# Weighted values two units at a time, ahead of every second unit's scores, with the stage's work placed by a table

## The chip, the cores and the metric

The kernel runs on one core of one Trainium2 chip. The metric is the device time of one execution in microseconds. The core has five engines with a queue of instructions each, which they work off in order: TensorE (PE, matrix products; its weight loads are listed apart as PEld), VectorE (DVE), ScalarE (ACT), GpSimd (POOL) and SyncE (SP), which here issues all DMA transfers. Engines wait for each other by semaphores. Products land in PSUM, an accumulator memory of eight banks (0 to 7 in the code, `PS[:, bank, :]`); a bank has to be read out by ACT or DVE before PE may use it for something else.

## The reference

One sequence of 2048 rows of 512 numbers, in bfloat16. `xn` is the normalized `x`; an attention branch A and an MLP branch B both start from it, and the output is `x + A * silu(B)`.

```python
xn = _layernorm(x)
# A: 32 heads of 16; a row attends to itself and 7 earlier rows, 2 apart
W, dil = 8, 2
qkv = (xn @ wqkv)...                       # q, k, v per head
idx = pos[:, None] - (jnp.arange(W) * dil)[None, :]
logits = jnp.einsum("bhsd,bhswd->bhsw", q, kg) * Dh ** -0.5
attn = softmax(where(idx >= 0, logits, -1e9))
A = jnp.einsum("bhsw,bhswd->bhsd", attn, vg)... @ wo
# B
h = gelu(_layernorm(xn) @ w1)              # then shifted by 1 or 2 rows, by quarters of the columns
x1 = xn + h_shifted @ w2
B = x1 + gelu(_layernorm(x1) @ w3) @ w4    # w3: 512 x 1376, w4: 1376 x 512
return x + A * silu(B)
```

## The kernel before

Rows attend to rows of their own parity alone, so the rows are kept as two halves (`p` = 0, 1) of 1024 even or odd rows. The first 106 us load, normalize and project: queries, keys (`kM`), values, which are written to DRAM (`v_d`), and the MLP as far as the hidden activations (`h3a`, `h3b`). What the change touches is the stage behind that, a loop over `NU` = 18 units, nine to each half, of 114 rows each. The names in it:

- `scores(n)` (S in what follows): 32 products on row tiles 32*128 of TensorE into PSUM banks 0 to 3 (L682), then one `Exp` of ACT (L689) into `prob`. The next unit's scores need that Exp to be done.
- `band(n)`: DVE takes the minimum of `prob` with a mask (L694), which leaves the eight wanted keys of each row.
- `values(n)`: 32 products of `prob` with value rows on column tiles 128*32 (L708) into bank 4 (`O_ps`), 16 products for the softmax denominators into bank 5 (L718), and a copy of bank 4 by ACT into `oT` (L723). It runs for unit n-2, right behind the scores of unit n, until unit 15, where two units' values are caught up, each apart.
- `load_va(n)`: SP loads the unit's value rows from `v_d` into one of `NV` = 3 places of the tile `ring` (L671). A place is free once the values of three units ago are done. `ring` takes the memory of `w3_sb`, so the first loads come behind the last product with w3.
- `inverse()`, `write_rec(b)`, `read_rec(b, ...)`, `apply(b, ...)`: for a batch of four units DVE takes the reciprocal of the denominators (L730), SP writes it to DRAM (two transfers, L739) and reads it back spread over partitions (two, L742), and DVE multiplies `oT` with it (L755). They also lie on SP's one queue.
- `w4_take(k)`: k of the 176 products with `w4` (L820). Eleven of them make one `Group` for 128 rows: the group takes a bank from `free`, which starts as `[6, 7]`, at its first product and puts it back at its last; DVE adds the bank to `x1` (L833), ACT takes a tanh (L840) and DVE makes the gate of it (L842). TensorE's time between the small blocks is filled with these, by shares worked out from `W4`, `kept_back` and the unit's number.
- `small_g`: a group of four products in each unit, for the queries of the second half in units 0 to 7 (L851, copied by ACT at L857), later for the output product with `wo` (L877, copied at L884; `finals` then multiplies with the gate, L892, and adds to the output rows `xo`, L896). They use the banks of `free`, too.
- `load_xo`, `flush_stores`, `load_wo`: loads of `x` rows into `xo` (L522), stores of finished rows (L784), the load of `wo` (L781), all on SP's queue.

`pin` keeps every engine's instructions in the order in which the code issues them: what the loop issues first, its engine does first. Behind the loop stand the last unit's values, the last eight products with `w4`, and the output groups 1 to 7 of the second half.

Of the kernel before, what the change touches and what calls it, by code (L numbers as in the profile page):

```python
# [8 lines left out]
AF = mybir.ActivationFunctionType  # L9
# [11 lines left out]
def kernel(  # L21
# [19 lines left out]
    def pin(ins):  # L41

        return tc.keep_in_program_order(ins)

    P = 128
    S = 2048
# [77 lines left out]
    load_x(2, 0, 2)  # L124
    load_x(2, 2, 2)
    w2_sb = b4([P, ND, D], "w2_sb")
    WS = 5664
    w3_sb = wpl.tile([P, WS], BF16, name="w3_sb", tag="w")[:, 0 : ND * F].rearrange("p (dt f) -> p dt f", f=F)
    w4_sb = wpl.tile([P, WS], BF16, name="w4_sb", tag="w")[:, 0 : NF * D].rearrange("p (ft n) -> p ft n", n=D)
    pin(ACT.preload_act_table_set("sqrt_and_others"))  # L130
# [81 lines left out]
    class Norm:  # L212
# [24 lines left out]
        def apply(self, lo, hi):  # L237
            for j in range(lo, hi):
                pin(DVE.tensor_scalar(
                    out=self.dst[:, j, :], in0=self.src[:, j, :], scalar1=self.mv[:, j, 0:1],  # L240
                    scalar2=self.rstd[:, j : j + 1], op0=ALU.subtract, op1=ALU.mult,
                ))
# [414 lines left out]

    pin(ACT.preload_act_table_set("exp_and_others"))
    ring = wpl.tile([P, WS], BF16, name="ring", tag="w")
    NV = 3  # L660
    va_r = ring[:, 0 : NV * 2 * D].rearrange("p (s b d) -> p s b d", s=NV, b=2)
    rr_t = ring[:, NV * 2 * D : NV * 2 * D + 4 * ND * NQ].rearrange("p (j a q) -> p j a q", j=4, a=ND)
    S_ps, O_ps, D_ps = PS[:, 0:4, :], PS[:, 4, :], PS[:, 5, 0:NQ]
# [4 lines left out]
    def load_va(n):  # L668
        p, u = n // UP, n % UP
        src = ap_of(v_d[p][:], [[D, P], [QB * 2 * D, 2], [1, D]], (NQ * u + 1) * 2 * D)  # L670
        pin(SP.dma_start(out=va_r[:, n % NV], in_=src))  # L671

    probs = {}

    def scores(n):
        p, u = n // UP, n % UP
        for dt in range(ND):
            for k in range(2):
                b = 2 * u + k
                for rg in range(4):  # L680
                    r = slice(32 * rg, 32 * rg + 32)
                    pin(PE.matmul(  # L682
                        S_ps[:, rg, (2 * dt + k) * QB : (2 * dt + k + 1) * QB],
                        lhsT=kM[p][r, dt, b * QB + 1 : b * QB + 65, :].rearrange("p k e -> p (k e)"),
                        rhs=qT[p][r, dt, b * QB : (b + 1) * QB], start=True, stop=True,
                        tile_position=(32 * rg, 0),
                    ))
        pr = probs[n] = b4([P, 4, ND * NQ], "prob")
        pin(ACT.activation(pr, S_ps[:, :, 0 : ND * NQ], AF.Exp, scale=SCALE))  # L689

    def band(n):
        pr = probs[n]
        f = pr.rearrange("p r x -> p (r x)")
        pin(DVE.tensor_tensor(out=f, in0=f, in1=maskb[:], op=ALU.min))  # L694
        if n % UP == 0:
            z = pr[0:14].rearrange("p r (a k q) -> p (r a) k q", k=2, q=QB)
            pin(DVE.memset(z[:, :, 0, 0:7], 0.0))

    def values(n):
        p, u = n // UP, n % UP  # L700
        if u == 0:
            oT[p] = b8([P, ND, MQ], f"oT{p}")
        pr = probs.pop(n)
        for dt in range(ND):
            for k in range(2):
                for rg in range(4):
                    x = (2 * dt + k) * QB
                    pin(PE.matmul(  # L708
                        O_ps[32 * rg : 32 * rg + 32, x : x + QB],
                        lhsT=va_r[:, n % NV, k, 32 * (4 * dt + rg) : 32 * (4 * dt + rg) + 32],  # L710
                        rhs=pr[:, rg, x : x + QB], start=True, stop=True, tile_position=(0, 32 * rg),
                    ))
        b = batch_of[n]
        lo, hi = batches[b]
        st = den_st if hi - lo == 4 else den_s2
        for dt in range(ND):
            for rg in range(4):
                pin(PE.matmul(  # L718
                    D_ps[32 * rg : 32 * rg + 32, :], lhsT=st[:, 4 * (n - lo) + dt, :],
                    rhs=pr[:, rg, dt * NQ : (dt + 1) * NQ], start=(n == lo and dt == 0),  # L720
                    stop=(n == hi - 1 and dt == ND - 1), tile_position=(0, 32 * rg),
                ))
        pin(ACT.activation(  # L723
            oT[p][:, :, u * NQ : (u + 1) * NQ], O_ps[:, 0 : ND * NQ].rearrange("p (a q) -> p a q", q=NQ), AF.Copy
        ))

    def inverse():
        rec = small_t("rec", [P, NQ], BF16)
        with nc.allow_low_precision("bf16 weights"):
            pin(DVE.reciprocal(out=rec, in_=D_ps))  # L730
        return rec
# [192 lines left out]
    def flush(q):  # L924
        while q:
            q.pop(0)()
# [4 lines left out]

    open_w4 = [g for g in w4s]

    unit = {"left": 0, "given": 0}

    def w4_take(k, extra=()):


        k = min(k, unit["left"])
        while k > 0 and open_w4:  # L940
            t = open_w4[0].take(k)
            k -= t
            unit["left"] -= t
            unit["given"] += t
            if open_w4[0].at == open_w4[0].n:
                open_w4.pop(0)
                if extra:
                    extra.pop(0).all()
                    if unit["left"] <= 5:
                        k = unit["left"] = 0  # L950

    HEAD, LAST = 6, 8
    W4 = 16 * NF - LAST - HEAD
    xo_at = {9: (1, 0), 11: (1, 6), 12: (1, 2), 13: (1, 4)}

    kept_back = {n: (2 * n - 9) // 5 for n in range(5, 15)}
    ends = {5: 0, 9: 1, 13: 2, 16: 3}
    load_va(0)
    for n in range(NU):
        now["n"] = n  # L960
        q = W4 * (n + 1) // NU + 2 * (n < 4) - kept_back.get(n, 0) - unit["given"]
        extra = small_g.get(n, [])

        early = n < 8
        if n == 0:
            unit["left"] = HEAD
            w4_take(HEAD)
            unit["given"] = 0
        unit["left"] = q

        for j in range(2):
            if n == NU - 1:
                read_rec(3, 2 * j, 2)
            elif n - 1 - j in ends:
                read_rec(ends[n - 1 - j], 2 * j, 2)
        if n == 15:
            values(13)
        scores(n)
        if 1 <= n < 16:
            band(n - 1)  # L980
        if n >= 2 and n != 15:
            values(n - 2 if n < 16 else n - 1)
        if n + 1 < NU:
            load_va(n + 1)
        if n == 4:
            load_wo()
        if n != 16:
            flush(finals)
        if n in (5, 16):
            recs[ends[n]] = inverse()  # L990
            write_rec(ends[n])
        if n == 17:
            free += [2, 3]
            pin(ACT.preload_act_table_set("silu_and_others"))
        w4_take(5 if n == 15 else q // 3)
        late = list(gates)
        gates.clear()
        flush(tanhs)
        if n == 15:
            values(14)  # L1000
            apply(2, 0, 2)
        if n == 17:
            band(n)
        w4_take((q - 5) // 2 if n == 15 else q // 3, extra if early else [])
        if n in (9, 13):
            recs[ends[n]] = inverse()
            write_rec(ends[n])
        if n < 15:
            flush(late)
        if 15 <= n < 17:  # L1010
            band(n)
        if n == 16:
            flush(finals)
        w4_take(unit["left"], extra if early else [])
        if not early and n < NU - 1 and 0 < open_w4[0].at < 5:
            unit["left"] = 5 - open_w4[0].at
            w4_take(unit["left"])
        for j in range(2):
            if n < 15 and n - 2 - j in ends:
                apply(ends[n - 2 - j], 2 * j, 2)  # L1020
        if n == 16:
            apply(2, 2, 2)
        if n >= 15:
            flush(late)
            flush(gates)
        while extra:
            extra.pop(0).all()

        if n in xo_at:
            load_xo(*xo_at[n])  # L1030
        if n in (12, 14):
            flush_stores(n - 1)

    n = NU
    now["n"] = n
# [3 lines left out]
        apply(3, j, 2)  # L1039
    flush(gates)  # L1040
    flush(tanhs)
    unit["left"] = 16 * NF
    w4_take(16 * NF)
    flush(tanhs)
    banks = [PS[:, i, :] for i in range(2)]
# [52 lines left out]
```

## Time and profile before

| | us |
|---|---|
| median of 3 runs | 190.67 (190.53 to 191.05) |
| the profiled execution | 190.66 |
| its span in the trace | 188.9 |
| start of the first w4 product, start of the unit loop on TensorE | 106.62 |
| start of the last block of output products (44 of L877) | 178.30 |
| their end | 184.55 |

TensorE's granted clock is 1.0 throughout. A page lists for each engine the time for which it was busy, the chain of work that ended last, and groups of equal instructions by line; the timeline lists instructions in order of time, where neighbours of one line are merged, with "[idle before <-releaser]" behind those that the engine waited for. Lines of the profile before are those of the code before; the changed code has the same instructions one line further down from `values` to the loop (L709 for L708, L821 for L820, and so on).

### The profile page before, as it was taken

How to read it: one execution, taken by the hardware profiler on the slowest of the kernel's cores; microseconds unless marked ns; L12 is line 12 of the kernel's file. 1: busy time of each engine (PE TensorE's matmuls, PEld its weight loads, DVE VectorE, ACT ScalarE, POOL GpSimd, SP SyncE). 2: the span in 40 equal slices, each digit the busy share in tenths (PEclk: the TensorE clock that was granted, in tenths of full speed). 3: DMA queues.
4: the chain of work that ended last, by engine and by line, in shares of the span. 5: the costliest groups of instructions: out<-in, count | busy, mean ns of one | idle time of the engine just before them, and what ended most of it. 6: DMA issues, size and time to landing. Idle time of an engine off the chain costs nothing.

```text
span 188.9 us, 5343 instructions
## 1 busy us (share of the span) xinstructions
PE 183.3 (97%) x2276; PEld 89.1 (47%) x2276; DVE 116.1 (61%) x230; ACT 131.9 (70%) x156; POOL 21.0 (11%) x60
## 2 busy tenths in 40 slices
PE   7999999999999999999999999999999999999990
PEld 2564444444444444444444444454455454545570
DVE  5897768260661996863000045565589799789893
ACT  7399858795169046156587688699678788867981
POOL 3025655000020022043000000000000000000000
PEclk9999999999999999999999999999999999999999
DMA  4999574679604699404700141252622684752136
GB/s 125 361 353 303 118 162 86 113 249 295 234 0 86 197 305 167 100 11 102 233 3 0 34 136 57 58 168 79 209 60 71 186 247 133 219 164 60 56 103 233
DMA packets 39348, 27.75 MB, mean 147 GB/s; under 512 B 18068, under 2 KB 38812, under 8 KB 39324
## 3 DMA queue, kind: packets, MB, share of 16 engines
q1 hardware_dynamic: 39324, 27.41, 53.4%
q8 instruction: 18, 0.29, 0.7%
q14 instruction: 6, 0.05, 0.1%
HBM read 17.14 MB, written 6.59 MB: 126 GB/s over the span
## 4 chain that ended last, share of the span: by engine, by line
PE 91%; DVE 4%; DMA 1%; ACT 1%; issue 0%
PE PS L820 21%; PE PS L490 18%; PE PS L342 16%; PE PS L381 7%; PE PS L446 7%; PE PS L877 4%; PE PS L851 4%; PE PS L708 3%; PE PS L682 3%; PE PS L718 2%; PE PS L332 2%; DVE sg L892 1%; PE PS L508 1%; DVE xo L896 1%; DMA xn<-in_A_x_dram 1%; DVE l1s L223 1%
## 5 line engine op out<-in xcount | busy, mean ns | idle before, releaser
L490 PE MATMUL PS<-x1nT,w_sb 128*128 128x512 bf16 x160 | 35.0, 379 | 0.0
L820 PE MATMUL PS<-w_sb,h3a 128*128 128x512 bf16 x128 | 32.0, 380 | 0.0
L689 ACT ACTIVATE prob<-PS 128x1824 bf16<-128x1824 f32 x18 | 30.4, 1686 | 1.6 <-PE PS L682 1.6
L833 DVE TENSOR_TENSOR xn<-PS,xn 128x512 bf16<-128x512 f32 x15 | 10.4, 691 | 31.8 <-PE PS L820 31.6
L495 ACT ACTIVATE h3a<-PS 128x1024 bf16<-128x1024 f32 x16 | 16.4, 1024 | 19.1 <-PE PS L490 19.1
L490 PEld LDWEIGHTS <-w_sb 128*128 128x128 bf16 x160 | 15.6, 98 | 19.0 <-issue 0.4
L694 DVE TENSOR_TENSOR prob<-prob,maskb 128x1824 bf16<-128x1824 bf16 x18 | 19.8, 1101 | 1.6 <-ACT prob L689 1.6
L372 ACT ACTIVATE kM<-PS,em 128x1024 bf16<-128x1024 f32 x12 | 16.0, 1405 | 2.1 <-PE PS L342 2.1
L820 PEld LDWEIGHTS <-h3a 128*128 128x128 bf16 x128 | 11.3, 97 | 13.0 <-issue 0.2
L454 DVE TENSOR_TENSOR xn<-PS,xn 128x1024 bf16<-128x1024 f32 x8 | 9.6, 1214 | 11.8 <-PE PS L446 11.8
L877 PE MATMUL PS<-wo_sb,oT 128*128 128x512 bf16 (+1 forms) x80 | 15.5, 336 | 0.0
L884 ACT ACTIVATE sg<-PS 128x512 bf16<-128x512 f32 (+1 forms) x20 | 10.1, 512 | 7.1 <-PE PS L877 6.8
L381 PE MATMUL PS<-wv_sb,xnT 128*128 128x512 bf16 x64 | 15.0, 379 | 0.0
L342 PE MATMUL PS<-xnT,wk_sb 128*128 128x512 bf16 x64 | 14.8, 379 | 0.0
L342 PE MATMUL PS<-xn2T,w_sb 128*128 128x512 bf16 x64 | 14.6, 379 | 0.0
L446 PE MATMUL PS<-w_sb,hT 128*128 128x512 bf16 x64 | 14.3, 379 | 0.0
L820 PE MATMUL PS<-w_sb,h3b 128*128 128x512 bf16 (+1 forms) x48 | 13.4, 380 | 0.0
L419 ACT ACTIVATE hT<-PS 128x1024 bf16<-128x1024 f32 x8 | 8.2, 1030 | 5.3 <-PE PS L342 5.3
L392 ACT ACTIVATE vst<-PS 128x1024 bf16<-128x1024 f32 x8 | 8.2, 1021 | 4.7 <-PE PS L381 2.9
L223 DVE BATCH_NORM_STATS2 l1s<-xn 128x6 f32<-128x512 bf16 x16 | 10.2, 680 | 1.1 <-DMA xn<-in_A_x_dram 1.0
L877 PEld LDWEIGHTS <-oT 128*128 128x128 bf16 x80 | 7.8, 98 | 6.0
L223 DVE BATCH_NORM_STATS2 l3s<-xn 128x6 f32<-128x512 bf16 x16 | 10.2, 682 | 0.2
(112 smaller groups left out, 239.6 us busy)
## 6 DMA issues: line engine op xcount, KB each, us to landing
ring<-v_d SPq DMA_DIRECT2D x18, 256.0 KB, 3.5
v_d<-vst SPq DMA_DIRECT2D x16, 256.0 KB, 3.2
xo<-in_A_x_dram SPq DMA_DIRECT2D x8, 256.0 KB, 3.8
ring<-rec_d SPq DMA_DIRECT2D x8, 228.0 KB, 3.8
out_dram<-xo SPq DMA_DIRECT2D x7, 256.0 KB, 3.3
xn<-in_A_x_dram SPq DMA_DIRECT2D x6, 256.0 KB, 5.0
w_sb<-in_B_w_dram SPq DMA_DIRECT2D x1, 1376.0 KB, 7.9
w_sb<-in_B_w_dram SPq DMA_DIRECT2D x1, 1280.0 KB
```

The lines of the kernel that those rows point to most:

```text
L223: pin(DVE.bn_stats(out=self.st[:, j, :], in_=self.src[:, j, :]))
L342: pin(PE.matmul(pt[:, b, :], lhsT=w[:, dt, nt * P : (nt + 1) * P], rhs=rhs[:, dt, :], start=(dt == 0), stop=(dt == ND - 1),))
L372: pin(ACT.activation(dst, pt, AF.Copy, scale=sc))
L381: pin(PE.matmul(pt, lhsT=xnT[p][:, dt, t * P : (t + 1) * P], rhs=wv_sb[:, dt, :], start=(dt == 0), stop=(dt == ND - 1),))
L446: pin(PE.matmul(pt[:, j, :], lhsT=w2_src(p, g, m0), rhs=w2_sb[:, g, :], start=(g == 0), stop=(g == ND - 1),))
L490: pin(PE.matmul(pt[:, b, :], lhsT=w3_sb[:, dt, ft * P : (ft + 1) * P], rhs=x1nT[:, dt, :], start=(dt == 0), stop=(dt == ND - 1),))
L495: pin(ACT.activation(t[:, o : o + 2, :], pt, AF.Gelu_apprx_tanh))
L689: pin(ACT.activation(pr, S_ps[:, :, 0 : ND * NQ], AF.Exp, scale=SCALE))
L694: pin(DVE.tensor_tensor(out=f, in0=f, in1=maskb[:], op=ALU.min))
L820: pin(PE.matmul(pt, lhsT=h3_of(c, ft)[:fs, jj * P : (jj + 1) * P], rhs=w4_sb[:fs, ft, :], start=(ft == 0), stop=(ft == NF - 1 and silu < 2),))
L833: pin(DVE.tensor_tensor(out=x_i, in0=pt, in1=x_i, op=ALU.add))
L877: pin(PE.matmul(pt[:, 0:W], lhsT=oT[p][:, dt, i * P : (i + 1) * P], rhs=wo["sb"][:, dt, c], start=(dt == 0), stop=(dt == ND - 1),))
```

## The change

`values` can take another bank than `O_ps`. The step Y (`value_pair`) runs the values of two units one behind the other; the second takes a bank from `free` and puts it back at once. Units 3, 5, 7, 9, 11, 13 and 15 begin with it, ahead of their scores, for the units n-3 and n-2; in unit 16 a pair for units 14 and 15 stands in the middle; unit 16's values follow the scores of unit 17, and unit 17's stand behind the loop, as they did. In units without Y the scores stand alone between products on the whole array. `ring` gets a fourth place (`NV` = 4), for which its memory grows from 5664 to 5920 elements per partition. Loads of value rows (D), w4 products (a number), masks (B), small groups (G), the steps of the reciprocals (I, R, A), loads and stores (X, O, W), tanh (T) and gates (L, M, F) come in the order that a table of 18 lines gives, in place of the shares and conditions. The number of w4 products in the loop stays at 168.

```diff
-    WS = 5664
+    WS = 5920
...
-    NV = 3
+    NV = 4
...
-    def values(n):
+    def values(n, bank=None):
         p, u = n // UP, n % UP
+        O_b = O_ps if bank is None else bank
...
                     pin(PE.matmul(
-                        O_ps[32 * rg : 32 * rg + 32, x : x + QB],
+                        O_b[32 * rg : 32 * rg + 32, x : x + QB],
...
         pin(ACT.activation(
-            oT[p][:, :, u * NQ : (u + 1) * NQ], O_ps[:, 0 : ND * NQ].rearrange("p (a q) -> p a q", q=NQ), AF.Copy
+            oT[p][:, :, u * NQ : (u + 1) * NQ], O_b[:, 0 : ND * NQ].rearrange("p (a q) -> p a q", q=NQ), AF.Copy
         ))
...
+    def w4_take(k):
         while k > 0 and open_w4:
-            t = open_w4[0].take(k)
-            k -= t
-            unit["left"] -= t
-            unit["given"] += t
+            k -= open_w4[0].take(k)
             if open_w4[0].at == open_w4[0].n:
                 open_w4.pop(0)
...
-    xo_at = {9: (1, 0), 11: (1, 6), 12: (1, 2), 13: (1, 4)}
-    kept_back = {n: (2 * n - 9) // 5 for n in range(5, 15)}
-    ends = {5: 0, 9: 1, 13: 2, 16: 3}
-    load_va(0)
+    xo_at = [(1, 0), (1, 6), (1, 2), (1, 4)]
+    steps_of = {k: [(b, j) for b in range(4) for j in range(2)] for k in "RA"}
+    order = {k: list(range(NU)) for k in "VBD"}
...
+    def value_pair():
+        values(order["V"].pop(0))
+        no = free.pop(0)
+        values(order["V"].pop(0), PS[:, no, :])
+        free.append(no)
...
+    step = {
+        "S": lambda: scores(n),
+        "V": lambda: values(order["V"].pop(0)),
+        "Y": value_pair,
+        "B": lambda: band(order["B"].pop(0)),
+        "D": lambda: load_va(order["D"].pop(0)),
+        "G": lambda: small_gs.pop(0).all(),
+        "T": tanh_all,
+        "L": lambda: flush(late),
+        "M": lambda: flush(gates),
+        "F": lambda: flush(finals),
+        "I": next_inverse,
+        "R": read_half,
+        "A": apply_half,
+        "X": lambda: load_xo(*xo_at.pop(0)),
+        "O": lambda: flush_stores(n - 1),
+        "W": load_wo,
+        "P": more_banks,
+    }
+    schedule = [
+        "6 D D D F 5 S T G 6",
+        "S 3 L 2 F B G T L",
+        "B S F 5 T 3 G L 3",
+        "Y D B S D F 2 T 1 L G 4",
+        "1 F 1 S B 3 T W L 4 G 1",
+        "Y S B D F I 2 D T L G",
+        "R 3 F S B 3 T 4 G L 6",
+        "Y R B S D D F 3 T 4 A G L",
+        "S F 1 B T 5 L 3 G A 3",
+        "Y S D B D F 2 T I 4 L G",
+        "S R T B F 6 L 6 G 4",
+        "R B Y S F D 2 D 5 L 3 T A",
+        "S B L T F 2 A O X G",
+        "Y S D B T D F L 5 I G X",
+        "B O R 6 F S 4 T 2 L G B 2",
+        "Y S R F 4 T B D 3 L A M",
+        "T G S 4 Y I X D 3 B 5 F G M",
+        "L R A R S X V 3 F P B 6 T M G L",
+    ]
+    load_va(order["D"].pop(0))
     for n in range(NU):
         now["n"] = n
-        q = W4 * (n + 1) // NU + 2 * (n < 4) - kept_back.get(n, 0) - unit["given"]
...
+        for k in schedule[n].split():
+            if k.isdigit():
+                w4_take(int(k))
+            else:
+                step[k]()
```

More of the change, by code (lines that the diff above doesn't have):

```diff
@@ L932 @@
     open_w4 = [g for g in w4s]
-    unit = {"left": 0, "given": 0}
-    def w4_take(k, extra=()):
-        k = min(k, unit["left"])
+    def w4_take(k):
         while k > 0 and open_w4:
-            t = open_w4[0].take(k)
-            k -= t
-            unit["left"] -= t
-            unit["given"] += t
+            k -= open_w4[0].take(k)
             if open_w4[0].at == open_w4[0].n:
                 open_w4.pop(0)
[L947 to L950, printed above, removed]
@@ L952, with tanh_all @@
-    HEAD, LAST = 6, 8
-    W4 = 16 * NF - LAST - HEAD
-    xo_at = {9: (1, 0), 11: (1, 6), 12: (1, 2), 13: (1, 4)}
-    kept_back = {n: (2 * n - 9) // 5 for n in range(5, 15)}
-    ends = {5: 0, 9: 1, 13: 2, 16: 3}
-    load_va(0)
+    xo_at = [(1, 0), (1, 6), (1, 2), (1, 4)]
+    steps_of = {k: [(b, j) for b in range(4) for j in range(2)] for k in "RA"}
+    order = {k: list(range(NU)) for k in "VBD"}
+    late = []
+    def tanh_all():
+        late.extend(gates)
+        gates.clear()
+        flush(tanhs)
@@ new lines, in next_inverse, with read_half, apply_half, more_banks @@
+    def next_inverse():
+        b = len(recs)
+        recs[b] = inverse()
+        write_rec(b)
+    def read_half():
+        b, j = steps_of["R"].pop(0)
+        read_rec(b, 2 * j, 2)
+    def apply_half():
+        b, j = steps_of["A"].pop(0)
+        apply(b, 2 * j, 2)
+    def value_pair():
[3 more added lines that the diff above has]
+        free.append(no)
+    def more_banks():
+        free.extend([2, 3])
+        pin(ACT.preload_act_table_set("silu_and_others"))
@@ new lines @@
+    small_gs = [g for n in sorted(small_g) for g in small_g[n]]
+    step = {
[17 more added lines that the diff above has]
+    }
@@ L959 @@
+    schedule = [
[18 rows of a table added]
+    ]
+    load_va(order["D"].pop(0))
     for n in range(NU):
         now["n"] = n
-        q = W4 * (n + 1) // NU + 2 * (n < 4) - kept_back.get(n, 0) - unit["given"]
[L962 to L1030, printed above, removed]
@@ L1031 @@
-        if n in (12, 14):
-            flush_stores(n - 1)
+        for k in schedule[n].split():
[3 more added lines that the diff above has]
+                step[k]()
     n = NU
@@ L1041 @@
     flush(tanhs)
-    unit["left"] = 16 * NF
     w4_take(16 * NF)
```

## The prediction

> **What bounds the kernel now.** I read the page first: its busy line, its chain and the chain's lines.
>
> ```profile
> PE 183.3 (97%) x2276; PEld 89.1 (47%) x2276; DVE 116.1 (61%) x230; ACT 131.9 (70%) x156; POOL 21.0 (11%) x60
> ...
> PE 91%; DVE 4%; DMA 1%; ACT 1%; issue 0%
> ```
>
> TensorE (PE) is busy for 97% of the span and makes 91% of the chain that ended last; no other engine comes near. So the second view is PE's timeline over the stage that the change touches, the 18 units from 106.6 us on. One ordinary unit (number 7) and unit 15, whose order differs:
>
> ```profile
> 136.29 1.03 PE L851 MATMUL PS<-xnT,wq_sb 128*128 128x512 bf16 x4
> 137.25 0.40 PE L682 MATMUL PS<-qT,kM 32*128 32x57 bf16 x32
> 137.59 0.42 PE L708 MATMUL PS<-prob,ring 128*32 128x57 bf16 x32
> 137.83 0.38 PE L718 MATMUL PS<-prob,den_st 128*32 128x114 bf16 x16
> 138.15 1.90 PE L820 MATMUL PS<-w_sb,h3a 128*128 128x512 bf16 x8
> ...
> 162.62 0.42 PE L708 MATMUL PS<-prob,ring 128*32 128x57 bf16 x32
> 162.87 0.39 PE L718 MATMUL PS<-prob,den_st 128*32 128x114 bf16 x16
> 163.19 0.40 PE L682 MATMUL PS<-qT,kM 32*128 32x57 bf16 x32
> 163.53 0.60 PE L820 MATMUL PS<-w_sb,h3a 128*128 128x512 bf16 x2
> ```
>
> The columns are start, length, line. No row has an idle time behind it: PE goes from block to block without waiting for anybody, so only PE's own sequence can shorten the stage. I call a scores block S (L682, 32 matmuls), the values block V (L708), the denominators D (L718), and everything on the whole array F (L820, L851, L877). Within F the starts follow each other at 0.217 us. The cost sits at the seams. Read start by start, the interval from the last matmul of one block to the first of the next is 0.311 us for F to S or V (0.094 over the normal 0.217), 0.118 for S to V, 0.116 for S to F, 0.147 for D to F, 0.146 for D to S (once, in unit 15), and only 0.020 for V to D. Within D, from one group of four column tiles to the next, it is 0.039. V and D share a tile form, 128*32; each seam that changes the form costs about 0.1 us more.
>
> Third, what the other engines need, since with PE full any new wait of PE is a loss:
>
> ```profile
> L689 ACT ACTIVATE prob<-PS 128x1824 bf16<-128x1824 f32 x18 | 30.4, 1686 | 1.6 <-PE PS L682 1.6
> L723 ACT ACTIVATE oT<-PS 128x456 bf16<-128x456 f32 x18 | 10.0, 554 | 0.0
> L884 ACT ACTIVATE sg<-PS 128x512 bf16<-128x512 f32 x12 | 7.2, 597 | 6.8 <-PE PS L877 6.8
> L857 ACT ACTIVATE qT<-PS 128x512 bf16<-128x512 f32 x8 | 4.8, 596 | 4.7 <-PE PS L851 4.6
> ```
>
> These are groups of the stage's ScalarE (ACT) instructions; the number behind the busy time is the mean in ns. Last, the view of L671, the value-row loads:
>
> ```profile
> DMA to landing us min/median/max: 2.9/3.5/5.4
> ```
>
> **Time base.** The profiled execution took 190.66 us (span 188.9 and 1.76 around it); the median of the runs shown is 190.67, so sums made on the one hold for the other.
>
> **Part 1: fewer seams.** The amount of matmul work is the same: 176 products on w4 (168 inside the loop, 8 behind, in both), 8 query groups, 18 S, 18 V, 18 D. The number of block boundaries in the loop is the same too; their kinds change. F to S or V: 20 before, 20 after. Of the 36 others, before: 15 S-V, 3 S-F, 17 D-F, 1 D-S. After: 1 S-V (unit 17), 17 S-F, 3 D-F, 7 D-S (units 3 to 15, odd) and 8 D-V inside the pairs; unit 16's pair stands apart from its scores. Before: 15 x 0.118 + 3 x 0.116 + 17 x 0.147 + 0.146 = 4.76 us. After, without the D-V seams: 0.118 + 17 x 0.116 + 3 x 0.147 + 7 x 0.146 = 3.55 us. The D-V seam is in no row. Bounds: 0.020 (V-D) and 0.147 (as if the form changed). I take 0.039, D's own step from one group to the next, since D and V keep the form. 8 x 0.039 = 0.31, so the seams fall by **0.90 us** (1.05 to 0.03 at the bounds). The Trainium skill, page "TensorEngine Tiling (Array Packing)", section "Key Properties", says that a change of the tiling mode drains TensorE and a change of tile alone does not; the V-D row of 0.020 agrees, and by the rule D-V is the cheap kind.
>
> **Part 2: a wait that goes.** In unit 1, L820 starts at 110.38 after four L851 from 109.44: 0.943 instead of 0.864, as the add L833 (0.69 us from 109.64) frees the bank only at 110.33. After the change the first w4 group ends ahead of unit 0's scores and its add has the time of S and four query products. **-0.08 us.**
>
> **Part 3: new waits.** The second V of a pair takes a bank of the two (6, 7) that w4 groups and the small groups rotate through; PE must wait for that bank's last reader, and whoever takes it next waits for the copy L723. ACT is in order, and a following instruction starts about 0.11 us before its predecessor's listed end. Three places come out short; I count from the last start of the small group ahead, with 0.42 us from there to the copy's start (0.38 matmul, 0.04 hand-over) and 0.05 back to PE (the 110.33 to 110.38 above).
> - Unit 5: after unit 4's query group PE has one product and V, D: 0.217 + 0.311 + 0.247 + 0.209 = 0.98. The bank is free at 0.42 + 0.60 + 0.05 = 1.07. **+0.09.**
> - Unit 16's output group takes the bank of a w4 group whose last product lies five starts back, 5 x 0.217 = 1.09 us; its add needs 0.42 + 0.69 + 0.05 = 1.16. **+0.08.**
> - Unit 16: a new w4 group starts three products behind the pair, in the pair's second bank. ACT: small copy, then Exp at 0.90, copies L723 at 2.47 and 2.92, end 3.47, with 0.05 at 3.52. PE: 0.311 + 0.334 (S) + 0.962 (4 F and the seam) + 0.247 + 0.209 + 0.247 + 0.317 (the pair) + 0.651 = 3.28. **+0.24.**
> Together +0.41; bounds 0 (should the banks be free sooner) and 0.7 (four more bank changes have under 0.02 us to spare, and an ACT hand-over of 0.1 instead of 0.05 brings these to light). I take 0.41.
>
> **Part 4: what costs nothing, and its cover.** Probabilities live a unit longer; Exp follows two copies now, but scores(n+1) still find S's banks free, at the least with 0.1 us (units 1 to 2, 5 to 6); without that cover PE pays the difference. The loads go out in pairs, two units or more ahead: each has over 8 us from issue to its V, except the last. That one, load 17, stands in SP's queue behind unit 16's reciprocal, its two writes (0.65 us each) and an xo load (0.5): issue about 2.9 us behind the pair's end. V(17) follows the pair's end by 6.8 us (12 products with the 0.24 wait, two small groups, S, V and D with their seams; the last six products of unit 17 included). So it has 3.8 us, where before it was issued at 165.2 for a V at 175.4. At the median of 3.5 it is hidden; a later landing goes one to one into PE, as V(17), its denominators and all products stand behind it. Behind the waiting reciprocal write SP holds that load and the reads of the reciprocals, which are read no later than before against PE; DVE has 39% idle for them. The xo loads move from units 9 to 13 to units 12 to 17; the last is issued near 173, and the add of its rows stands near 183 now. POOL has nothing in this stage. Behind the loop all is as before.
>
> **Sum.** 190.66 - 0.90 - 0.08 + 0.41 = 190.09, say **190.1 us**.
>
> **Rivals.**
> 1. *The new waits do not come.* If the copies free the banks in time, 190.66 - 0.98 = 189.7. For it: all three are differences of chains of five to eight terms, the first two under 0.1 us. Against it: the same arithmetic gives unit 1's 0.08 as the trace has it.
> 2. *D-V costs like a change of form.* 8 x (0.147 - 0.039) = 0.86 of the gain is gone; the pairs come later, so that unit 5's wait goes and unit 16's halves: 190.66 - 0.03 - 0.08 + 0.2 = 190.8. For it: weights of another tile are loaded. Against it: V-D does that too, for 0.020.
> 3. *The last value rows come late (the other side).* The wait at V(17) is the landing less 3.8 us. It eats the gain from a landing of 4.4 on and makes the kernel slower by 0.57 from 4.9; at the longest in the trace, 5.4, it is 1.6 us and the time 191.7. For it: the cover shrinks from 10 to 3.8 us, and an xo load is ahead in the queue with two reads behind. Against it: long landings in the trace stood amid reads and stores; behind two writes it took 3.3 (issue at 161.85), in quiet stretches some 3 to 3.6, though once 4.2 (114.98). That page "DMA: Bandwidth & Descriptors", section "Latency and other measured facts", of the Trainium skill lets HBM latency grow to 2 us under load speaks for this rival; the trace's 2.9 to 5.4 agrees with such a spread.
>
> **Chances.** A difference within 0.3% (0.57 us, that is 190.10 to 191.24) is about what a measurement of this kernel can't tell from none. Forecast 0.58, rival 1 0.18, rival 2 0.10, rival 3 0.14. The forecast lies on the bound, so it gives half to faster (0.29) and half to the same (0.29); rival 1 is faster (0.18), rival 2 the same; rival 3 splits by its landing, 0.12 slower and 0.02 the same. Faster 0.47, same 0.41, slower 0.12. The range goes from 189.5 (seams at 0.020, no waits) to 190.9, which holds rival 2 and a landing up to 4.6; the forecast's own is 189.8 to 190.4.
>
> **What would show it.** The timeline should have D-V intervals near 0.04; PE's interval over 0.217 ahead of the second V of unit 5, of unit 16's L878 and of its second w4 group, with releasers ACT, DVE, ACT; L671's last landing before V(17). The start of unit 17 after unit 0 tells seams and waits from the last load. I am wrong if pairs show a seam of 0.1 us inside, if PE waits elsewhere in the loop, or if the end behind the loop is longer.

## The result and the profile after

| | before | after |
|---|---|---|
| median of 6 runs each, side by side, us | 190.66 (190.38 to 191.05) | 196.01 (194.68 to 196.50) |
| the profiled execution | 190.66 | 196.04 |
| its span | 188.9 | 194.1 |

The ratio is 1.0268, 95% interval 1.0232 to 1.0304: the changed kernel is slower by 5.1 us. Forecast were 190.1 us and a range of 189.5 to 190.9; the time lies outside it, on the side of rival 3.

The page of the changed kernel, TensorE's busy line and the chain of work that ended last:

```profile
PE 182.3 (94%) x2250; PEld 89.9 (46%) x2276; DVE 116.1 (60%) x230; ACT 133.1 (69%) x156; POOL 20.3 (10%) x60
...
PE 74%; DMA 10%; DVE 7%; ACT 4%; issue 2%; SPq 1%; ACTq 0%
```

TensorE had 91% of the chain; now it is 74%, and DMA has 10%. (2250 of 2276 products are recorded; where a record is missing, the timeline shows "issue" waits of about 0.16, which are none.) The chain's pieces in order of time (start, duration, what) and TensorE's timeline at the same place, the end of the unit loop:

```profile
172.45 6.13 DMA ring<-v_d
178.58 0.04 issue
178.62 0.58 PE PS L709 x31
```

```profile
174.94 1.03 PE L878 MATMUL PS<-wo_sb,oT 128*128 128x512 bf16 x4
178.62 0.58 PE L709 MATMUL PS<-prob,ring 128*32 128x57 bf16 x32 [2.65 <-DMA ring<-v_d]
179.01 0.57 PE L719 MATMUL PS<-prob,den_s 128*32 128x114 bf16 x16
179.91 1.91 PE L821 MATMUL PS<-w_sb,h3a 128*128 128x512 bf16 x4 [0.33 <-issue]
```

Load 17, the last value rows, is issued at 172.45 and lands 6.13 us later. TensorE stands 2.65 us for it ahead of V(17), the values of unit 17. The kernel before ran these blocks without a wait:

```profile
175.38 0.42 PE L708 MATMUL PS<-prob,ring 128*32 128x57 bf16 x32
175.62 0.38 PE L718 MATMUL PS<-prob,den_s 128*32 128x114 bf16 x16
175.94 1.25 PE L820 MATMUL PS<-w_sb,h3a 128*128 128x512 bf16 x5
```

Then something follows that no text ahead of the result spoke of: V(17) and its denominators take 0.58 and 0.57 where they took 0.42 and 0.38, and four products take 1.91 where before five took 1.25. The table by stretches of time (length; busy time and count of PE, PEld, DVE, ACT, POOL; granted clock; DMA share; GB/s) says why:

```profile
109.50:175.90 66.40, 64.51 (x1602) 33.59 (x1617) 49.48 (x75) 54.72 (x66) 0.00 (x0) 1.00 0.42 123
175.23:178.65 3.42, 0.76 (x8) 0.15 (x9) 0.94 (x2) 2.58 (x4) 0.00 (x0) 1.00 0.88 259
178.60:182.10 3.50, 3.14 (x54) 1.65 (x56) 2.43 (x5) 0.55 (x1) 0.00 (x0) 0.51 0.02 9
182.10:187.00 4.90, 4.90 (x36) 2.99 (x35) 3.03 (x8) 3.61 (x8) 0.00 (x0) 1.00 0.07 20
```

The granted clock is 0.51 in the 3.5 us behind the wait and 1.00 in front and behind. TensorE's other waits from 100 us on:

```profile
PE PS L709 <- DMA ring<-v_d: 2.7, 1, 2.7
...
PE PS L878 <- DVE xn L834: 0.3, 1, 0.3
```

Unit 7, which the prediction showed, now begins with a pair. Its seams are as forecast: from the last start of the first L719 to the first of the second L709 it is 0.04.

```profile
133.28 0.42 PE L709 MATMUL PS<-prob,ring 128*32 128x57 bf16 x32
133.53 0.39 PE L719 MATMUL PS<-prob,den_st 128*32 128x114 bf16 x16
133.74 0.41 PE L709 MATMUL PS<-prob,ring 128*32 128x57 bf16 x32
133.97 0.39 PE L719 MATMUL PS<-prob,den_st 128*32 128x114 bf16 x16
134.29 0.40 PE L682 MATMUL PS<-qT,kM 32*128 32x57 bf16 x32
```

Of the ScalarE groups shown of before, the Exps (1691 ns, 1686 before) and the copies of values keep their durations. What grows is the waiting ahead of these copies, 4.3 us in place of 0.0. Of this, 1.4 us stand at V(17). The other 2.9 stand ahead of earlier copies; the run E8 below has them too, and TensorE waits there for nothing over 0.15 us.

```profile
L724 ACT ACTIVATE oT<-PS 128x456 bf16<-128x456 f32 x18 | 9.4, 555 | 4.3 <-PE PS L709 4.3
```

**Where the time went.** The two traces, cut at the starts of weight loads, with three experiments of the next section (E1: load 17 earlier; E8: the same with all instructions shifted by 204 places; E9: the kernel before, shifted alike), in us:

| | before | after | E1 | E8 | E9 |
|---|---|---|---|---|---|
| start of the first w4 product | 106.40 | 106.81 | 106.65 | 107.03 | 107.07 |
| from there to the scores of unit 6 | 22.36 | 22.35 | 22.56 | 22.13 | 22.34 |
| to the scores of unit 15 | 34.43 | 34.30 | 34.31 | 34.42 | 34.43 |
| to the scores of unit 17 | 8.37 | 8.62 | 9.07 | 8.15 | 8.38 |
| to V(17) | 3.81 | 6.54 | 3.82 | 3.81 | 3.81 |
| to the last weight load | 8.79 | 10.36 | 8.79 | 8.79 | 8.79 |
| to the end | 4.69 | 5.15 | 5.06 | 4.46 | 4.45 |

After against before: 0.41 later at the start, 0.11 more in the three loop stages, 2.73 at V(17), 1.57 behind it, 0.46 at the very end, together 5.28, the difference of the spans. Products are spread otherwise over the units, so one stage alone isn't like for like; the sum over the loop is. 4.30 of 5.28 us stand at V(17) and right behind it.

### The profile page after: what moved, and what is told of

Same layout as the page of the kernel before. It is cut to its first block, busy times and chain, and to the rows that moved or that the text cites. A ratio compares the mean times of both kernels' runs of the same rounds, so it can differ in the third digit from the quotient of the medians.

```text
span 194.1 us, 5313 instructions
## 1 busy us (share of the span) xinstructions
PE 182.3 (94%) x2250; PEld 89.9 (46%) x2276; DVE 116.1 (60%) x230; ACT 133.1 (69%) x156; POOL 20.3 (10%) x60
## 4 chain that ended last, share of the span: by engine, by line
PE 74%; DMA 10%; DVE 7%; ACT 4%; issue 2%; SPq 1%; ACTq 0%
PE PS L490 18%; PE PS L342 16%; PE PS L821 14%; PE PS L446 7%; PE PS L381 6%; PE PS L852 3%; DMA ring<-v_d 3%; DMA ring<-rec_d 3%; DMA xn<-in_A_x_dram 2%; PE PS L682 2%; PE PS L878 2%; PE PS L709 2%; DVE sg L893 1%; DVE xo L897 1%; PE PS L508 1%
## 5 line engine op out<-in xcount | busy, mean ns | idle before, releaser
L689 ACT ACTIVATE prob<-PS 128x1824 bf16<-128x1824 f32 x18 | 30.4, 1691 | 2.4 <-PE PS L682 1.9
L834 DVE TENSOR_TENSOR xn<-PS,xn 128x512 bf16<-128x512 f32 x15 | 10.3, 685 | 31.6 <-PE PS L821 31.6
L878 PE MATMUL PS<-wo_sb,oT 128*128 128x512 bf16 (+1 forms) x80 | 15.5, 336 | 0.3 <-DVE xn L834 0.3
L724 ACT ACTIVATE oT<-PS 128x456 bf16<-128x456 f32 x18 | 9.4, 555 | 4.3 <-PE PS L709 4.3
L878 PEld LDWEIGHTS <-oT 128*128 128x128 bf16 x80 | 7.7, 97 | 6.6 <-issue 0.8
```

Source lines behind the costliest of these rows:

```text
L834: pin(DVE.tensor_tensor(out=x_i, in0=pt, in1=x_i, op=ALU.add))
L878: pin(PE.matmul(pt[:, 0:W], lhsT=oT[p][:, dt, i * P : (i + 1) * P], rhs=wo["sb"][:, dt, c], start=(dt == 0), stop=(dt == ND - 1),))
```

## The experiments

**E1: load 17 one unit earlier.** Only the place of one D changes.

```diff
-        "Y S R F 4 T B D 3 L A M",
-        "T G S 4 Y I X D 3 B 5 F G M",
+        "Y S R F 4 T B D D 3 L A M",
+        "T G S 4 Y I X 3 B 5 F G M",
```

> The changed kernel with one edit: the load of unit 17's value rows is issued in unit 15, behind the load for unit 16, instead of behind unit 16's reciprocal writes and an xo load. Theory 'late rows' (the loss is TensorE's wait for that load, 2.7 us in the trace, and the half clock that follows it): no wait ahead of V(17), granted clock 1.0, time 190.2 to 190.9. Rival 'the pairs' (values two at a time, their banks and the table's order cost it all over the loop): the time stays above 193.

Measured: 192.22 us (192.03 to 192.67), ratio 1.0080 (1.0054 to 1.0106), between the two times that were expected. V(17) starts without a wait and the clock behind it is full: 3.8 of the 5.3 us are gone with one transfer's place.

```profile
176.41 0.42 PE L709 MATMUL PS<-prob,ring 128*32 128x57 bf16 x32
```

But E1 is still 1.5 us over the kernel before, where the sum of the prediction has it 0.57 under. The lists of TensorE's weight loads show part of the rest. Units 5 and 16 of E1:

```profile
126.39 0.23 PEld L682 LDWEIGHTS <-kM 32*128 32x128 bf16 x23
126.97 0.14 PEld L682 LDWEIGHTS <-kM 32*128 32x128 bf16 x9 [0.36 <-issue]
...
167.94 0.18 PEld L719 LDWEIGHTS <-den_st 128*32 128x32 bf16 x9
168.57 0.12 PEld L719 LDWEIGHTS <-den_st 128*32 128x32 bf16 x7 [0.46 <-issue]
```

One block of 32 weight loads, which no semaphore parts, is cut in 23 and 9, another of 16 in 9 and 7, by 0.36 and 0.46 us in which TensorE waited for nothing that the trace shows. Besides, the second of unit 16's two output groups (L878) waits 0.5 us for L834, which stands in DVE's queue behind an `apply` that waits 1.3 us for its read of the reciprocals.

**E2: the kernel before with load 17 as late as the change has it** (between the two reads of reciprocals in unit 17).

```diff
         for j in range(2):
             if n == NU - 1:
+                if j == 1:
+                    load_va(NU - 1)
                 read_rec(3, 2 * j, 2)
...
-        if n + 1 < NU:
+        if n + 1 < NU - 1:
             load_va(n + 1)
```

> The kernel before with one edit: the load of unit 17's value rows is issued between the two reads of the reciprocals in unit 17, some 2.4 us ahead of V(17), instead of in unit 16. No pairs, no table. Theory 'late rows': TensorE waits 1 to 3.5 us ahead of V(17); if the wait is over 2 us the granted clock falls below 1.0 behind it; time 192 to 196. Rival 'the pairs': no more than 191.3, as the load's latency of 3.5 us less 2.4 us is the most that it could cost.

Measured: 192.92 us (192.58 to 193.68), ratio 1.0119 (1.0086 to 1.0152). Chain and timeline of this run:

```profile
173.73 3.91 DMA ring<-v_d
```

```profile
177.68 0.42 PE L708 MATMUL PS<-prob,ring 128*32 128x57 bf16 x32 [1.60 <-DMA ring<-v_d]
```

The late load alone costs the kernel before some 2 us, with an ordinary landing of 3.91. In the profile V(17) comes 1.67 us later behind unit 17's scores; the loop also begins 0.60 later there, ahead of the edit. A stand of 1.60 us doesn't halve the clock.

**E3: the four xo loads back in units 9 and 11 to 13**, load 17 as late as in the changed kernel.

```diff
-        "Y S D B D F 2 T I 4 L G",
+        "Y S D B D F 2 T I 4 L G X",
...
-        "R B Y S F D 2 D 5 L 3 T A",
+        "R B Y S F D 2 D 5 L 3 T A X",
...
-        "T G S 4 Y I X D 3 B 5 F G M",
-        "L R A R S X V 3 F P B 6 T M G L",
+        "T G S 4 Y I D 3 B 5 F G M",
+        "L R A R S V 3 F P B 6 T M G L",
```

> The changed kernel with the four xo loads back in units 9, 11, 12 and 13, where the kernel before has them; unit 17's row load stays behind the reciprocal writes, but no xo load stands ahead of it or behind the reads. If the traffic around that load makes it late (landing 6.1 us, where other loads took 2.7 to 4.7), it is issued 0.5 us sooner and lands after 3 to 4.5 us: the wait at V(17) falls from 2.7 to 0 to 1.3 us, the clock stays 1.0, time 190.5 to 192.5. If its place alone matters, or a transfer of another kind holds it up, the wait stays over 1.5 us and the time over 193.

Measured: 191.45 us (190.49 to 192.36, 10 executions), ratio 1.0034 (1.0013 to 1.0056). Load 17 is issued at 172.38, as in the changed kernel. By the records of its 16 parts it lands 3.79 us later, and TensorE doesn't wait for it:

```profile
176.38 0.42 PE L709 MATMUL PS<-prob,ring 128*32 128x57 bf16 x32
```

So the place in time was tight, but it alone doesn't make the landing 6.13: without the two xo loads, one just ahead of it in the queue and one behind, the same load is there 2.3 us sooner. Which of the two matters, no run separates. The blocks of weight loads are cut again at the same two instructions, by 0.84 and 0.46 us.

**E4: the changed kernel with 12 constant products in the gap ahead of V(17).** They fill 2.75 us of TensorE's stand and nobody reads them.

```diff
     n = NU
     now["n"] = n
+    no = free.pop(0)
+    for i in range(12):
+        pin(PE.matmul(
+            PS[:, no, :], lhsT=ones_bf[:], rhs=ones_bf.unsqueeze(1).to_broadcast([P, TPC, P]),
+            start=True, stop=True,
+        ))
+    free.append(no)
     values(NU - 1)
```

> The changed kernel with 12 products of a constant on the whole array (2.6 us, into a free bank that nobody reads) put just ahead of V(17), where TensorE waits. The row load is as late as before, and the products fit into the wait. Theory 'the half clock follows the idle time': TensorE doesn't idle for long, the granted clock stays at 1.0 and the time falls by 1.2 to 1.8 us to some 194.4, although work was added. Rival 'the clock falls for another reason' (traffic, the end of the loop): 196 or more, clock 0.99 or less.

Measured: 194.04 us (193.70 to 194.90), ratio 1.0179 (1.0144 to 1.0215). V(17) waits for the load as long as ever, but the stretch behind it keeps its clock:

```profile
175.55 2.75 PE L1031 MATMUL PS<-ones_bf 128*128 128x512 bf16 x12
178.46 0.42 PE L709 MATMUL PS<-prob,ring 128*32 128x57 bf16 x32 [0.16 <-DMA ring<-v_d]
```

```profile
178.60:182.10 3.50, 3.34 (x68) 1.98 (x61) 2.65 (x5) 1.47 (x3) 0.00 (x0) 1.00 0.02 8
```

Added work makes the kernel 2.0 us faster at the median. From V(17) to the last weight load it is 8.79 us again, 10.36 in the changed kernel: the halved clock costs 1.57 us and comes of the stand. (The other 0.4 us is no more than the start and the end of the execution vary by; see "What stays open" below.)

**E5 and E6: every instruction of TensorE shifted.** The trace's DMA records hold 18 transfers of 16 KB on an instruction queue. Counted in the program, the instruction at which TensorE stops in units 5 and 16 is number 1987 and number 4035, eight times 256 apart, in E1 and E3 alike; and TensorE goes on 1.4 and 1.2 us after such a transfer has ended (E1: transfers 124.53 to 125.55 and 165.34 to 167.37, on at 126.97 and 168.57). That suggests that TensorE's program comes in pages of 256 instructions and that TensorE can reach a page before it is there. E5 is E1, E6 the kernel before, with tiny constant products at the start, which move everything behind them to other places: 114 in E5, 78 in E6 (which has 40 in place of the 58 below).

```diff
-    for i in range(10):
+    for i in range(9):
         pin(PE.matmul(
             PS[:, 6 + i % 2, :], lhsT=ones_bf[:], rhs=ones_bf.unsqueeze(1).to_broadcast([P, TPC, P]),
             start=True, stop=True,
         ))
+    for i in range(58):
+        rg = i % 4
+        pin(PE.matmul(
+            PS[32 * rg : 32 * rg + 32, 6, 0:QB], lhsT=ones_bf[:, 0:32], rhs=ones_bf[:, 0:QB],
+            start=True, stop=True, tile_position=(0, 32 * rg),
+        ))
```

> The kernel with unit 17's load early, and one edit at the very start: 9 instead of 10 warm-up products, and 58 tiny ones on column tiles (128*32, 57 columns, a constant), which shift all later TensorE instructions by 114 places; the loop is untouched. With the load early, TensorE still stood still twice without a semaphore, for 0.4 us amid unit 5's scores and 0.5 us amid unit 16's denominators, both times at a weight load whose number in the program is 2047 apart, 1.2 to 1.5 us behind the end of a 16 KB instruction transfer. Theory 'instruction supply' (256 instructions come as one page; a pair with scores uses a page up faster than the next one comes): the page ends now fall elsewhere, these two stops shrink to under 0.15 us each, no other stop over 0.3 us appears, and the time falls by 0.6 to 1.1 us to 191.1 to 191.6. Rival 'the stops belong to these blocks' (a data dependence, PSUM, the tile form): they stay, 192.2.

> The kernel before with 9 instead of 10 warm-up products and 40 tiny ones at the start, so that all later TensorE instructions stand 78 places further on; its loop is untouched. Theory 'instruction supply': page ends now fall behind the densest stretches of the loop (units 5 to 6 and units 11 to 13), stops of 0.3 to 0.8 us without a semaphore appear there, time 191.2 to 192.0. Rival: the loop is the same, so the time stays at 190.4 to 190.9.

Measured: E6 takes 192.17 us (191.97 to 192.44), ratio 1.0070 (1.0045 to 1.0095). Its loop is untouched, and yet two blocks are now cut, at numbers 2243 (at 130.66, by 0.20) and 3523, again on page ends:

```profile
156.60 0.26 PEld L714 LDWEIGHTS <-ring 128*32 128x32 bf16 x25
157.34 0.12 PEld L714 LDWEIGHTS <-ring 128*32 128x32 bf16 x7 [0.48 <-issue]
```

From the first w4 product to V(17) it is 69.86 us, 0.89 over the kernel before, as much as these two stops, which take 0.29 and 0.58 from one start to the next. The rest of E6's profiled time is 1.02 us by which its loop begins later, 0.9 of it waits of the first 40 us for DVE. So its time came near the expectation only partly for the reason that was given. In E5 the stop of unit 5 is gone, and the one at 4035 now falls on unit 16's scores (0.32). Its ten executions lie in two groups, three at 190.23 to 190.64 and seven at 192.11 to 194.26; the ratio, without the two over 193, is 1.0044 (1.0010 to 1.0078). The median, 192.45, is not below E1's, and no execution lies in the 191.1 to 191.6 that were expected: a miss. So the place in the program decides where TensorE can stop, but E5 doesn't show that the shift shortens E1. What puts an execution of E5 into one group or the other isn't in its one profile (of 190.64).

**E7: all of it together**, xo loads back, load 17 early, E5's shift (the edits of E1, E3 and E5).

> The changed kernel with all three causes taken away: unit 17's load in unit 15, the xo loads in units 9, 11, 12 and 13, and the shift of 114 instructions. If late rows, the half clock, late reads of the reciprocals and the instruction supply are all there is, what is left are the fewer seams and the new bank waits as predicted: 190.0 to 190.5, a little faster than the kernel before. If the pairs cost something else, it stays over 190.9.

Measured: 192.49 us (191.78 to 194.30), ratio 1.0098 (1.0063 to 1.0133), a miss. The profiled execution, of 194.30, has the largest stop of all, in a pair, and a half clock behind it:

```profile
155.49 0.17 PEld L725 LDWEIGHTS <-den_st 128*32 128x32 bf16 x10
157.70 0.11 PEld L725 LDWEIGHTS <-den_st 128*32 128x32 bf16 x6 [2.04 <-issue]
```

```profile
159.28:162.69 3.41, 3.41 (x10) 1.22 (x8) 1.11 (x1) 1.93 (x3) 0.00 (x0) 0.50 0.24 41
```

It stands at number 3523. The page ahead began at 153.08; the instruction transfer started only at 155.30, when the DMA engines had been 84% busy since 153, and ended at 156.30, 1.40 us before TensorE went on. An xo load put back beside it is part of that traffic.

**E8 and E9: a shift by 204 places**, for E1 (E8) and for the kernel before (E9), by eight warm-ups and 104 tiny products (against E5). By the traces no page of the loop is then run through in less than 3.4 us (E8) and 4.1 us (E9).

```diff
-    for i in range(9):
+    for i in range(8):
...
-    for i in range(58):
+    for i in range(104):
```

> The kernel before with eight warm-up products in place of ten and 104 tiny constant products behind them (32x57 results that nobody reads): every later PE instruction stands 204 places further on, and the loop is untouched. Theory (PE's instructions come in pages of 256, and a page that PE runs through in less than some 4 us lets it stop): with this shift no page of the loop is run through in under 4.1 us (3.7 before, 3.2 to 3.3 with the 78 places of the earlier shift), so no stop: 190.4 to 191.1, although two and a half times as many tiny products are added. Rival (the tiny products themselves, or the warm-up that they replace, cost the 1.5 us that the shift by 78 showed): 192 or more.

> The changed kernel with load 17 one unit earlier (as in the first experiment) and the same 204 places. Theory (page stops make most of what the first experiment left over): the stops of 0.42 in unit 5 and 0.5 in unit 16 go; the shortest pages, 3.4 us near unit 5 and 3.5 near unit 9, may give up to 0.4 each: 190.6 to 191.8, between no stop and both. Rival (what was left over is DMA or bank waits, wherever the pages fall): as the first experiment, 192.0 to 192.6.

Measured: E9 190.90 us (190.69 to 192.22), ratio 1.0029 (1.0004 to 1.0055); its loop stages equal those of the kernel before to 0.02 us (the table), and it begins 0.67 later. So the tiny products don't lengthen the loop, and the 0.89 us in that of E6, with 40 of them, came of the places. E8 takes 191.24 us (190.65 to 193.45), ratio 1.0047 (1.0020 to 1.0074): 1.0 us less than E1 at the median, with nine of ten executions below all of E1's. From the first w4 product to V(17) its profile has 68.51 us, against 69.76 in E1 and 68.96 in E9. Block by block, about 0.8 us less are the stops of units 5 and 16, and 0.65 less is the wait of unit 16's second output group, which E8's profile doesn't have (0.2 are lost elsewhere). That wait comes back in E10, with the same shift, so the shift alone doesn't account for it.

**E10, E11 and E12: the same 204 places with six warm-ups and 106 tiny products**: E10 as E8, E11 with the xo loads back, E12 the kernel before.

```diff
-    for i in range(8):
+    for i in range(6):
...
-    for i in range(104):
+    for i in range(106):
```

> The kernel before with six warm-up products in place of ten and 106 tiny constant products: the same 204 places as before, with less of them at the start (with eight and 104 the loop began 0.67 us later than without). Both theories: the loop as in the kernel before, 68.97 us from its first product to V(17); 190.3 to 190.7 if the start is level again, 190.9 if it isn't.

> The changed kernel with load 17 one unit earlier and the same six warm-ups and 106 tiny products. Theory (the grouping gains what the prediction's sum says, 0.57 less the 0.3 by which unit 16's output group waits longer than forecast, once the pages don't stop PE): about 0.45 under the control with the same places (68.5 us from the loop's first product to V(17), as its sister with eight warm-ups had): 189.8 to 190.4. Rival (the grouping gains nothing lasting; its shorter pages find some other place to stop in): level with the control or up to 0.5 above it, 190.5 to 191.2.

> As the run above, and the four xo loads back in units 9 and 11 to 13. If the reads of the reciprocals come in time without the xo loads beside them, unit 16's output group waits 0.08 instead of 0.4: 189.5 to 190.1. If the xo loads delay a page in units 9 to 13 as they did with the other shift (2.1 us at place 3522), 191 or more.

Measured: E12 191.66 us (190.59 to 193.34), ratio 1.0051 (1.0025 to 1.0077); E10 191.39 (191.21 to 192.29), 1.0045 (1.0030 to 1.0061); E11 191.26 (190.27 to 192.00), 1.0025 (1.0008 to 1.0041). E12's and E10's expectations failed, E10 a little above both of its ranges, and E11's 191 or more came without the large stop that it was tied to (its one profile, of 190.27, shows no stop over 0.4). The control's miss says most. The profiled execution of E12, of 193.34, at the same places as E9:

```profile
160.11 0.28 PEld L688 LDWEIGHTS <-kM 32*128 32x128 bf16 x29 [0.42 <-issue]
160.94 0.10 PEld L688 LDWEIGHTS <-kM 32*128 32x128 bf16 x3 [0.55 <-issue]
...
165.11 0.17 PEld L688 LDWEIGHTS <-kM 32*128 32x128 bf16 x16
166.31 0.17 PEld L688 LDWEIGHTS <-kM 32*128 32x128 bf16 x16 [1.02 <-issue]
```

(The 0.42 ahead of a first row is a load waiting for the products ahead, as everywhere in the loop. A third stop, of 0.22, is at 139.18.) Without the stops these pages would have lasted 5.4 and 4.3 us, longer than the 3.7 that the kernel before runs through unharmed. But their transfers started 3.73 and 2.92 us after the page ahead had begun, 1.17 and 1.13 in E9. From 154.92 to 158.60, between the start of that page and the transfer, the trace shows no instruction packet, and value rows, an xo load and a store held the DMA engines for 79% of the time. So the length of a page doesn't decide alone; the start of the transfer that feeds it does, and that differs from execution to execution.

## Why the prediction was wrong

**Part 4 failed: "a later landing goes one to one into PE", with a cover of 3.8 us and a landing of 3.5.** Three of its sizes were off. The cover was 3.45 us: load 17 was issued at 172.45, 3.6 us behind the pair instead of 2.9, and V(17) could have started at 175.90. The landing was 6.13, outside the 2.9 to 5.4 of the trace of before, and 6.23 in E4; without the xo loads about it, it was 3.91 (E2) and 3.79 (E3). The longest landing of one trace was no bound either: load 16 took 5.99 in the changed kernel, loads 16 and 17 took 6.28 in E1, early enough to cost nothing. The prediction named the xo load ahead in the queue as a point for rival 3, and then took the landing of the quiet stretches. And one to one is too little: 2.65 us of standing cost 1.57 us more, by the clock (E4). Rival 3 had the mechanism and the place; its worst price, 1.6 us, was that of the longest landing seen, without the clock.

**Part 4 failed a second time: the reads of the reciprocals are "read no later than before against PE".** The first read of the third batch, issued at 162.43, lands after 6.00 us, where it took 3.24 before. DVE waits 0.8 us for it in the changed kernel (1.3 in E1, 1.1 in E10, none in E8). Behind that wait stands the add L834, which frees the bank of unit 16's second output group, and this group starts 0.47 us late (0.65 in E1, 0.55 in E10, 0 in E8, from start to start). The sum has nothing for it: the 0.08 of Part 3 is the unit's first output group. The page's median from issue to landing for these reads is 5.6 us, 3.8 before.

**A term was missing: TensorE's instructions.** The sum priced what TensorE does, not that its program must be there. V and D of two units and one S are (64 + 32) x 2 + 64 = 256 instructions, a whole page within 1.4 us, where S, V and D took 160 in 0.9. In the changed kernel itself the stops are small (0.1 in unit 5, 0.2 in unit 16); in E1 and E3 they are 0.4 to 0.8 in each of these units. The kernel before runs close to such stops, too: a shift by 78 places made them (E6). Shown is that the stops sit on page ends, move with the program and end 1.2 to 1.6 us behind a transfer. That dense pairs make them likelier is argued from the count, and no run tried it alone. Density alone isn't enough: in unit 9 the changed kernel runs through a whole page in 1.6 us (141.0 to 142.6) without a stop; in the long page ahead of it two transfers had ended, at 136.58 and 140.69.

**Part 1 was right.** Inside five of the eight pairs the D-V step is 0.035 to 0.041 (taken: 0.039). Unit 5's is 0.121 with the wait that was forecast for it, unit 16's 0.058, and unit 3's 0.151, which is 0.040 in E1 and E8. No pair shows a change of form. In E8, where every product is recorded, the seams that Part 1 adds up take 4.07 us, 0.16 of it waits, and 4.73 in the kernel before: 0.82 less without the waits, where 0.90 was forecast. Rival 2 is out.

**Parts 2 and 3 were right.** Unit 1's wait is gone. Unit 5's second V waits 0.08 (forecast 0.09), unit 16's first output group 0.08 (0.08). The new w4 group of unit 16 starts 3.22 us behind the scores in E8 and in E10, by the forecast's terms 3.21; the wait itself is only 0.04 and 0.18 there (forecast 0.24), because a stop within the second V, of 0.2 and 0.1, takes up the rest of the same time. Rival 1 is out. So is the net sum borne out for the loop: 68.51 in E8 against 68.97 before is -0.46, with a stop of 0.1 elsewhere in it, against -0.57 forecast. It closes in E1 as well: -0.57, stops of 0.44 and 0.50, 0.65 at unit 16's second output group, and 0.24 off for the wait that the second stop covers, give +0.78; measured is +0.79. Whole executions don't show the gain reliably: E8's median is 0.34 over E9's, E10's 0.27 and E11's 0.40 under E12's.

**What stays open.** The 0.41 us at the start and 0.46 at the end of the changed kernel are not the change's, as far as the traces show. E1, E3 and E4, whose code ahead of the loop is that of the changed kernel, begin 0.25 and 0.11 later and 0.04 earlier than the kernel before, and E2, whose code there is that of the kernel before, 0.60 later. At the end, 3.47 us pass from the last add to the end of the span, behind the last stores, 3.01 before and 2.77 in E4. What delays an instruction transfer within busy DMA, and so why one execution of E12 takes 190.6 and another 193.3, isn't settled. No version of the changed kernel beats the kernel before; the nearest is E11, with the ratio 1.0025.

## What to carry to other kernels

Price a moved load by the landings of loads that have the same neighbours in the queue, and don't take the longest landing of one trace for a bound (5.4 us before, up to 6.3 in the runs here). Price a stand of TensorE twice: its length, and the half clock that followed here behind 2.65 and 2.0 us, though not behind 1.60. When a rearrangement should save tenths in a kernel that is bound by TensorE, look for blocks cut in two with no releaser: TensorE can reach instructions that aren't there yet, and moving all of them by some places tells this from a wait for data. A control with the same shift belongs beside every such run, and more than one profile of it, because the stops vary between executions.

## What the runs showed of the hardware

**The clock.** It halves for exactly one stretch of 3.41 us and then returns: 178.645 to 182.06 in the changed kernel, 159.28 to 162.69 in E7. In the 3.42 us ahead TensorE was not wholly idle, but busy for 0.76 us (second row of the stretches above), in E7 for 1.52 us. The Trainium skill, page "TensorE: Matmul & The Clock Gate", advises in its section "Why this matters for your kernels" against idle gaps over about 3 us; here 2.65 us and a stop of 2.0 sufficed, and 1.60 (E2) did not.

**The supply of instructions.** The runs show stops of 0.1 to 2.0 us at ends of pages of 256 instructions, with TensorE going on 1.2 to 1.6 us behind the end of a 16 KB transfer that itself takes 0.9 to 2.0 in the loop. The Trainium skill, page "Runtime: NRT & Kernel Launch", section "Instruction fetch mechanics", has the blocks of 16 KB and 256 instructions, which the runs bear out, and calls the cost of crossing a boundary "mostly hidden"; in this loop it isn't, as E6 and E12 show.

**A late piece of a load.** Of load 17's 16 parts in the changed kernel 15 had reported by 176.73, 4.28 us after the issue, and the last at 178.58: one part made 1.85 of the 2.65 us that TensorE stood (in E4 the last came 1.89 behind). In both runs a 16 KB transfer of instructions ran amid the load (175.39 to 176.54 in the changed kernel); in E3, where the last part came only 0.50 behind, it began when 15 parts were there. The 14 traces hold 363 value-row loads and reads of reciprocals with all parts recorded. In 104 of them no such transfer lay between the issue and the 15th part, and the last part came over 1 us behind the 15th in none; in 219 it lay there for 0.5 us or more, and the last part was that late in 96. The 15th part comes after 3.1 us at the median in both. So the two go together; that the instructions hold up the load's part is likely, but no run tries it alone.
